# Attention values of five sequence halves loaded by GpSimd's queue, and the first operand pair read into another pool

## The chip, the cores and the metric

One core of a Trainium2 chip runs the whole program. The metric is the time of one execution in microseconds (us). The engines are named as in the profile: PE (TensorE matmul; PEld its weight loads), DVE (VectorE), ACT (ScalarE), POOL (GpSimd) and SP (SyncE, which here issues DMAs and computes nothing).

## What is computed

A block-local attention is followed by two feed-forward layers, all in float32 with a residual of the rounding carried in a second operand.

```
# q, k, v: [4, 8, 768, 64]; mem_k, mem_v: [4, 8, 8, 64]
for each chunk c of 32 queries:
    keys = 8 memory rows + 16 rows to the left + the chunk + 8 rows to the right
    a = softmax(q_c @ keys^T / 8);  out_c = a @ values        # per batch and head
x = out as [3072 tokens, 512]
h = x @ w_in;  g = h * clip(h + 3, 0, 6) / 6;  x = g @ w_out          # 512 -> 2048 -> 512
h = x @ w_in2; g = leaky_relu(h, 0.01);        out = g @ w_out2       # 512 -> 2048 -> 512
```

## The kernel before

**Attention.** The tokens are eight halves j = 0 to 7 of 384 tokens (half a batch's sequence). Each half has two units, `unit(j, quad, ...)`, of four heads. A unit loads queries and keys (`load_qk`, line 491, two DMAs of 448 KB), copies the keys into windows (`windows`), makes scores on PE (line 544), softmax on DVE and ACT, multiplies by the reciprocal of the sums (`norm`, line 598, on POOL or DVE), transposes on PE (line 602), and multiplies by the values on PE (line 634). The values are loaded by `load_v`: for each of two pairs of heads six DMAs, four of 84 KB (line 502) and two of 24 KB (line 504), in pieces of 512 bytes; so a unit has twelve such DMAs. Halves 0 and 1 are loaded in other forms (`load_whole`, `half_unit`). The result of a unit goes to operand tiles or, from half 2 on in part, through `attended` in memory (line 707).

**Feed-forward.** Tokens are blocks of 512. Blocks 0 and 1 are done plainly (lines 998 and 1047). The later blocks are taken in pairs, p = -2 and -1 for layer 1 and p = 0, 1, 2 for layer 2, by a scheme of seven products instead of eight (lines 1322 and 1490). `x_pair(p, ...)` makes the operands of a pair: `x_quarter` reads four tiles `b11`, `b12`, `b21`, `b22` (line 1126, `src`, 256 KB each) for each of two quarters, forms sums and differences on DVE, and splits each operand into two parts on ACT and DVE (lines 341 and 344, helpers `copy` and `minus`). For p = -2 the tiles come from `attended`.

**Places.** Tiles live in pools with a fixed number of places. Pool "w" has 33 places of 4 KB for each partition; weights, rings of kept sums (`kept1i` and others, line 1265), and operands share it. Pool "a" has 4 places; it holds queries and keys of halves 3 to 7, and for halves 6 and 7 also values and softmax tiles; `src` of `x_quarter` is there too. A load waits until a place is free.

**Order.** Every piece of work is a `Task` with a priority key and a cost for each engine that may do it. `schedule` simulates the engines with these costs and writes each engine's instructions in the order in which the simulation started them. On the chip each engine then runs its list in order, and waits on semaphores. So a cost or an engine that is changed for one task can change the order of everything behind it. For a DMA the planner takes 500 ns on SP and 1000 ns on POOL for each issue, and a landing later:

```
ISSUE = {"SP": 500.0, "POOL": 1000.0}
STARTS, LANDS, SURE = 1900.0, 500.0, 1500.0
...
                    for _ in range(pick.issues):
                        at = max(at, lanes[e].pop(0)) + ISSUE[e]
                        wire = max(wire, at + STARTS) + d / pick.issues
                        lanes[e].append(wire + LANDS)
...
                    push(wire + LANDS + (SURE if pick.allocs else 0.0), "done", (pick, e))
```

`norm` is offered to POOL first, and DVE takes it where POOL would end over 2.5 us later than DVE. In a unit from half 3 on, `load_v` comes after both `windows`; the loads of the next unit's queries and keys come after this unit's scores (halves 3 to 5, `ROOMY`) or after its first exponentials and both `load_v` (halves 6 and 7). Units of halves 6 and 7 begin after the last operand of `x_pair(-2)`.

Of the kernel before, what the change touches and what calls it, by code (L numbers as in the profile page):

```python
# [17 lines left out]
B, H, S, D, NMEM = 4, 8, 768, 64, 8  # L18
# [7 lines left out]
NC = G // CHUNK  # L26
# [30 lines left out]
RATE_QK, RATE, RATE_V, COLD = 380.0, 220.0, 300.0, 1.1  # L57
# [198 lines left out]
def tile_attn_moe_moe2(ctx: ExitStack, tc: tile.TileContext, raw, w1i, w1o, w2i, w2o, out):  # L256
    nc = tc.nc
# [24 lines left out]
    def make(b, kind=None):  # L282
        if b.tag in ("hx", "y") and b.tag not in pools:

            (attention if b.tag == "hx" else begin).close()
            pools[b.tag] = (ctx.enter_context(tc.tile_pool(name=b.tag, bufs=places[b.tag], space=PSUM, side="right" if b.tag == "hx" else "left")), [128, 512], F32)
        pool, shape, dt = pools[b.tag]
        if kind is not None:
            shape, dt = kind
        b.t = pool.tile(shape, dt, tag=b.tag, name=b.tag)  # L290
        return b.t
# [20 lines left out]
    def act(n, fixed=90.0):  # L312
        return fixed + 0.855 * n
# [13 lines left out]
    def dma(nbytes, rate=250.0):  # L327
        return nbytes / rate
# [3 lines left out]
    def add(fn, opts, key, **kw):  # L332
        t = Task(fn, opts, key, **kw)
        tasks.append(t)
        return t
# [129 lines left out]
    def unit(j, quad, key, tag, own=False, direct=False, loads=None):  # L465
# [7 lines left out]
        v = [Buf("w" if own or roomy else "a") for _ in range(2)]  # L473
        mx, s = Buf("mx"), Buf("mx")
        ps = pt = pv = Buf(tag)
        plain = own and j < 2
# [12 lines left out]
        def load_qk(i):  # L489
            def fn(eng):  # L490
                nc.sync.dma_start(out=make(qk[i], ([128, 2, QK], F32)), in_=both_groups(2 * quad + i))
            return fn

        def load_v(i):
            def fn(eng):
                make(v[i], ([128, 2, NC, 2 * D], F32))
                for par in range(2):
                    rows = of_raw(par, slice(0, KW), slice(QK, RAW))[i]
                    for g in range(2):
                        a = rows[g, NMEM:W]  # L500
                        there = bass.AP(tensor=a.tensor, offset=a.offset, ap=[a.ap[0], [CHUNK * a.ap[0][0], NC], a.ap[1]])
                        nc.sync.dma_start(out=v[i].t[par * D + NMEM:(par + 1) * D, g], in_=there)
                    mem = rows[0, :NMEM]
                    nc.sync.dma_start(out=v[i].t[par * D:par * D + NMEM].rearrange("r g c d -> r (g c) d"), in_=mem.unsqueeze(1).to_broadcast([NMEM, 2 * NC, 2 * D]))
            return fn

        def load_whole(i):

            def fn(eng):
                make(v[i], ([128, 6, 2 * D], F32))  # L510
                of = raw[b, 2 * quad + i, g0:g0 + 4, :, QK:RAW]
                nc.sync.dma_start(out=v[i].t[:, :4], in_=of.rearrange("g r d -> r g d"))
                for gp in range(2):
                    nc.sync.dma_start(out=v[i].t[gp * D:(gp + 1) * D, 4:], in_=of[2 * gp:2 * gp + 2, CHUNK:CHUNK + W].rearrange("g r d -> r g d"))
            return fn
# [198 lines left out]
        loads = loads or (key - 50, key - 50, key - 38, key - 38)  # L714
        l1 = [add(load_qk(i), {"SP": dma(128 * 2 * QK * 4, RATE_QK)}, loads[i], after=() if own else turn, allocs=[qk[i]]) for i in range(2)]
        t = [add(windows(i), ({"DVE": 850.0} if i or quad else {"ACT": 1050.0}) if j == 0 else {"ACT": 1050.0}, key - 30, after=[l1[i]], allocs=[kw[i]], uses=[qk[i]]) for i in range(2)]
        l2 = [add(load_whole(i) if plain else load_v(i), {"SP": dma(128 * 2 * NC * 512, RATE_V if plain else RATE)}, loads[2 + i], after=() if own else t, allocs=[v[i]], issues=3 if plain else 6, loads=plain) for i in range(2)]
        if plain:
            l2 = [add(memory(i), {"POOL": 1500.0}, key - 20, after=[l2[i]], uses=[v[i]]) for i in range(2)]
        t = marks["s", j, quad] = add(scores, {"PE": (COLD if direct else 1.0) * 1300.0}, key - 16, ins=192, after=t, allocs=[ps], uses=[*qk, *kw])  # L720
        scored = t
        if direct and quad in SHIFT:
            t = add(greatest, {"DVE": 2100.0}, key - 15, after=[t], allocs=[mx, e], uses=[ps])
            t = add(exp_all, {"ACT": act(2 * PAIRS * W)}, key - 13, after=[t], uses=[e])
            t = add(total, {"DVE": 1250.0}, key - 12, after=[t], allocs=[s], uses=[e])
        else:
            t = add(greatest, {"DVE": 1200.0}, key - 15, after=[t], allocs=[mx], uses=[ps])
            t = add(exp(0), {"ACT": 6 * 330.0}, key - 13, after=[t], allocs=[e, s], uses=[ps, mx])
            if not own:
                turn[:] = [scored] if roomy else [t, *l2]  # L730
            t = add(exp(1), {"ACT": 6 * 330.0}, key - 13, after=[t], uses=[ps, mx, e, s])
            t = add(total, {"DVE": 350.0}, key - 12, after=[t], uses=[s])
        t = add(norm, {"DVE": 900.0} if direct else {"POOL": 1800.0, "DVE": 900.0}, key - 11, after=[t], uses=[e, s])
        t = marks["t", j, quad] = add(transpose, {"PE": (COLD if direct else 1.0) * 600.0}, key - 7, ins=12, after=[t], uses=[e, ps])
        t = add(take_p, {"ACT": act(PAIRS * 128)}, key - 5, after=[t], uses=[pt, e])
        t = marks["v", j, quad] = add(values_whole if plain else values, {"PE": (COLD if direct else 1.0) * 1600.0}, key, ins=192, after=[t, *l2], uses=[e, *v, ps])
# [376 lines left out]
    def x_quarter(p, j, key, need):  # L1113


        a, b = pair_of(p)
        src = {n: Buf("a") for n in ("b11", "b12", "b21", "b22")}
        tt = Buf("w")
        ts = (tt, tt)
        got = {}  # L1120

        def load(n):
            t0 = blocks[a if n[2] == "1" else b][0]
            k = j + 2 * (n[1] == "2")
            r = src[n]
            got[n] = add(lambda e: nc.sync.dma_start(out=make(r, ([128, N], F32)), in_=spill[k, :, t0:t0 + N] if p >= 0 else attended[k, :, t0 - PLAIN * N:t0 - PLAIN * N + N]), {"SP": dma(N * 512, 330.0)}, key - 12, after=need[n[2] == "2"], allocs=[r])

        def sub(out, x, y, after, allocs=(), uses=()):
            return add(lambda e: minus(e, out(), x(), y()), {"DVE": dve(N)}, key, after=after, allocs=allocs, uses=uses)

        def parts_of(name, of, own, after):
            bufs = xop[p, name]
            first = xtask[p, name][0][:1], xtask[p, name][1][:1]
            hi = add(lambda e: copy(e, operand(p, name, 0, j).bitcast(F32R), of()), {"ACT": act(N)}, key, after=after + first[0], allocs=[] if first[0] else bufs[:1], uses=[own] + (bufs[:1] if first[0] else []))
            new = not first[1] and len(bufs) == 2
            lo = add(lambda e: minus(e, operand(p, name, 1, j).bitcast(F32R), of(), operand(p, name, 0, j).bitcast(F32)), {"DVE": dve(N)}, key, after=[hi] + first[1], allocs=bufs[1:] if new else [], uses=[own, bufs[0]] + ([] if new else bufs[1:]))
            xtask[p, name][0].append(hi)
            xtask[p, name][1].append(lo)
            return [hi, lo]

        def at(n):
            return lambda: src[n].t[:, :N]

        def t_at(i):
            return lambda: made(tt)[:, i]

        for n in src:
            load(n)

        def tt_kind():  # L1150
            for t in set(ts):
                make(t, ([128, 2, N], F32))

        def t_1(e):
            tt_kind()
            minus(e, t_at(0)(), src["b12"].t[:, :N], src["b11"].t[:, :N])

        d11 = parts_of("b11", at("b11"), src["b11"], [got["b11"]])
        if p >= 0:
            parts_of("b21", at("b21"), src["b21"], [got["b21"]])  # L1160
        t1 = add(t_1, {"DVE": dve(N)}, key, after=[got["b11"], got["b12"]], allocs=[*dict.fromkeys(ts)], uses=[src["b11"], src["b12"]])
        t2 = sub(t_at(1), at("b22"), t_at(0), [t1, got["b22"]], uses=[*ts, src["b22"]])
        parts_of("t2", t_at(1), ts[1], [t2])
        if p < 0:
            parts_of("b21", at("b21"), src["b21"], [got["b21"]])
        parts_of("t1", t_at(0), ts[0], [t1])
        t3 = sub(at("b12"), at("b22"), at("b12"), [t1, got["b22"]], uses=[src["b12"], src["b22"]])
        parts_of("t3", at("b12"), src["b12"], [t3])
        if p < 0 and j:
            key += 10  # L1170
        parts_of("b22", at("b22"), src["b22"], [got["b22"]])
        t4 = sub(at("b11"), at("b21"), t_at(1), [t2, t1, got["b21"], *d11], uses=[src["b11"], src["b21"], ts[1]])
        parts_of("t4", at("b11"), src["b11"], [t4])
# [404 lines left out]
    for f in range(KF):  # L1578
        for which, src, at in (("1i", w1i, pos_h["1", int(f >= KF // 2), f]), ("1o", w1o, pos_y["1", int(f >= KF // 2), f])):
            i = 2 * f + (which == "1o")  # L1580
# [33 lines left out]
    for kind, j, f, *n in seq2:  # L1614
        if kind == "p":
            p, i, n = j, f, n[0]
# [69 lines left out]
```

## Time and profile before

| | |
|---|---|
| median of 3 runs | 1046.41 us (1045.3 to 1048.34) |
| the profiled execution's own time | 1046.62 us |
| its span | 1044.8 us |
| PE busy | 1029.5 us, 99% of the span |
| DVE, ACT, POOL busy | 856.0, 694.8, 23.9 us (82%, 67%, 2%) |
| DMA | 220.50 MB, all but instruction fetches through one queue, 63.2% of 16 engines' span |

The span is the time from the first to the last instruction; the execution's own time is 1.8 us longer. A stretch's busy time is read against its length: what is missing is time in which that engine stood still. All DMAs of the kernel before are issued by SP; their issue instructions are not counted as busy.

### The profile page before, as it was taken

How to read it: one execution, taken by the hardware profiler on the slowest of the kernel's cores; microseconds unless marked ns; L12 is line 12 of the kernel's file. 1: busy time of each engine (PE TensorE's matmuls, PEld its weight loads, DVE VectorE, ACT ScalarE, POOL GpSimd, SP SyncE). 2: the span in 40 equal slices, each digit the busy share in tenths (PEclk: the TensorE clock that was granted, in tenths of full speed). 3: DMA queues.
4: the chain of work that ended last, by engine and by line, in shares of the span. 5: the costliest groups of instructions: out<-in, count | busy, mean ns of one | idle time of the engine just before them, and what ended most of it. 6: DMA issues, size and time to landing. Idle time of an engine off the chain costs nothing.

```text
span 1044.8 us, 20156 instructions
## 1 busy us (share of the span) xinstructions
PE 1029.5 (99%) x7476; PEld 846.7 (81%) x7476; DVE 856.0 (82%) x1422; ACT 694.8 (67%) x1478; POOL 23.9 (2%) x31
## 2 busy tenths in 40 slices
PE   7999999999999999999999999999999999999998
PEld 4788888877888888888888888888888888888887
DVE  6995897578998778699999898999476998566775
ACT  4886776555988554576786576776565874666753
POOL 3010000000000000000000000000000000000000
PEclk9999999999999999999999999999999999999999
DMA  9989787776888888664647884446342554432451
GB/s 259 298 237 323 256 286 236 247 256 215 276 288 292 292 279 278 245 217 127 212 135 268 291 286 162 147 158 218 117 167 81 177 194 153 169 114 95 148 181 61
DMA packets 127315, 220.50 MB, mean 211 GB/s; under 512 B 12528, under 2 KB 76016, under 8 KB 127216
## 3 DMA queue, kind: packets, MB, share of 16 engines
q1 hardware_dynamic: 127216, 219.20, 63.2%
q8 instruction: 59, 0.97, 0.4%
q14 instruction: 40, 0.33, 0.1%
HBM read 156.24 MB, written 62.91 MB: 210 GB/s over the span
## 4 chain that ended last, share of the span: by engine, by line
PE 85%; DMA 6%; DVE 4%; ACT 2%; SPq 2%; issue 1%; DVEq 0%; ACTq 0%
PE y L1322 17%; PE y L1490 12%; PE h L1322 11%; PE y L1047 10%; PE h L1490 8%; PE hx L1322 8%; PE hx L1490 8%; PE h L998 3%; PE h L1047 2%; DMA w<-in_raw 2%; DMA kept1i<-ys 1%; DMA a<-in_raw 1%; PE at L634 1%; DMA half<-ys 1%; PE at L544 1%
## 5 line engine op out<-in xcount | busy, mean ns | idle before, releaser
L344 DVE TENSOR_TENSOR w<-w 128x512 fp32r<-128x512 f32 (+2 forms) x393 | 323.3, 858 | 29.0 <-ACT w L341 28.4
L341 ACT CAST w<-w 128x512 fp32r<-128x512 f32 (+1 forms) x290 | 223.7, 805 | 12.5 <-DMA w<-floats 3.9
L1047 PE MATMUL y<-g,w 128*128 128x512 f32 (+1 forms) x540 | 124.9, 375 | 1.5 <-ACT g L341 0.6
L1322 PE MATMUL y<-w 128*128 128x512 f32 x516 | 124.2, 389 | 0.0
L1322 PEld LDWEIGHTS y<-w 128*128 128x128 f32 x516 | 96.7, 188 | 20.1
L1047 PEld LDWEIGHTS y<-g,w 128*128 128x128 f32 x540 | 94.0, 188 | 19.9 <-ACT g L341 1.4
L1490 PE MATMUL y<-w 128*128 128x512 f32 x384 | 90.3, 389 | 0.0
L341 ACT CAST g<-w 128x512 fp32r<-128x512 f32 x80 | 49.7, 623 | 58.3 <-PE y L1490 22.5
L1490 PEld LDWEIGHTS y<-w 128*128 128x128 f32 x384 | 72.1, 188 | 15.0
L1296 ACT ACTIVATE w<-w 128x512 f32<-128x512 f32 x72 | 45.3, 633 | 43.9 <-DVE w L1289 21.5
L998 PE MATMUL h<-xh,w 128*128 128x512 f32 (+1 forms) x288 | 66.0, 370 | 0.0
L344 DVE TENSOR_TENSOR g<-w,g 128x512 fp32r<-128x512 f32 x80 | 54.4, 689 | 11.5 <-ACT g L341 11.4
L1490 PE MATMUL h<-w 128*128 128x512 f32 x264 | 62.1, 389 | 0.0
L1322 PE MATMUL h<-xl,w 128*128 128x512 f32 x240 | 58.3, 391 | 1.2 <-ACT xl L341 1.2
L1490 PE MATMUL hx<-w 128*128 128x512 f32 x252 | 59.2, 389 | 0.0
L1490 PEld LDWEIGHTS h<-w 128*128 128x128 f32 x264 | 49.5, 188 | 10.3
L998 PEld LDWEIGHTS h<-xh,w 128*128 128x128 f32 x288 | 49.7, 188 | 9.0
L1490 PEld LDWEIGHTS hx<-w 128*128 128x128 f32 x252 | 47.3, 188 | 9.8
L1322 PEld LDWEIGHTS h<-xl,w 128*128 128x128 f32 x240 | 44.8, 188 | 11.3 <-ACT xl L341 1.6
L1322 PE MATMUL y<-xh,w 128*128 128x512 f32 x216 | 51.9, 389 | 0.0
L1367 DVE TENSOR_TENSOR w<-y,w 128x512 f32<-128x512 f32 x35 | 23.9, 687 | 29.9 <-PE y L1322 27.1
L1322 PEld LDWEIGHTS y<-xh,w 128*128 128x128 f32 x216 | 40.5, 188 | 8.5
(242 smaller groups left out, 1847.7 us busy)
## 6 DMA issues: line engine op xcount, KB each, us to landing
w<-kept2i SPq DMA_DIRECT2D x42, 512.0 KB
w<-kept2o SPq DMA_DIRECT2D x42, 512.0 KB
w<-kept1i SPq DMA_DIRECT2D x28, 512.0 KB
a<-in_raw SPq DMA_DIRECT2D x20, 448.0 KB
w<-in_w1i SPq DMA_DIRECT2D x16, 512.0 KB
w<-in_w1o SPq DMA_DIRECT2D x16, 512.0 KB
w<-in_w2i SPq DMA_DIRECT2D x16, 512.0 KB
w<-in_w2o SPq DMA_DIRECT2D x16, 512.0 KB
```

Of the source, the lines that this page charges most:

```text
L341: nc.scalar.copy(out, in_) if e == "ACT" else engine(e).tensor_copy(out=out, in_=in_)
L344: engine(e).tensor_tensor(out=out, in0=a, in1=b, op=ALU.subtract)
L544: nc.tensor.matmul(ps.t[h * CHUNK:(h + 1) * CHUNK, par, i * W:(i + 1) * W], qk[h // 2].t[r, gp, (h % 2) * G + c * CHUNK:(h % 2) * G + (c + ...
L634: nc.tensor.matmul(pv.t[(h % 2) * D:(h % 2 + 1) * D, par, (h // 2) * 2 * G + i * CHUNK:(h // 2) * 2 * G + (i + 1) * CHUNK], v[h // 2].t[r, ...
L998: nc.tensor.matmul(h.t[:, o:o + n], w.t[:, 1 if p == 1 else 0, k * 128:(k + 1) * 128], x[:, k, c0:c0 + n], start=(p == 0 and k == 0 and o ...
L1047: nc.tensor.matmul(bank(banks[d])[:, c0:c0 + n], w.t[:, 1 if p == 1 else 0, d * 128:(d + 1) * 128], g.t[:, 1 if p == 2 else 0, at:at + n], ...
L1296: return add(lambda e: nc.scalar.activation(out=at(), in_=at(), func=AF.Prelu, alpha=0.01), {"ACT": act(N)}, key, after=[after], uses=uses)
L1322: nc.tensor.matmul(bank(to), wt(l, o)[:, kt * 128:(kt + 1) * 128].bitcast(F32R), operand(p, name, 1 if q == 2 else 0, kt).bitcast(F32R), s ...
L1367: done[2] = add(lambda e: nc.vector.tensor_tensor(out=half_of(x, 0), in0=bank(bb), in1=ut.t[:, 0], op=ALU.add), low, key, after=[k, done[1 ...
L1490: nc.tensor.matmul(bank(to[d]), wt(1 if q == 1 else 0, o)[:, d * 128:(d + 1) * 128].bitcast(F32R), g.t[:, 1 if q == 2 else 0], start=(fres ...
```

## The change

Two edits. In units from half 3 on (`j >= 3 and not plain`; ten units, 120 DMAs) the two `load_v` tasks are issued by POOL, and the planner is told so: engine POOL, 1000 ns an issue, a rate of 300 bytes per ns on the wire instead of 220, and POOL counted as free after its last issue. In `x_quarter`, the four tiles of pair p = -2 take places of pool "w" instead of pool "a". The order is planned anew with both.

```diff
+        by_pool = j >= 3 and not plain
+
         def load_v(i):
...
-                        nc.sync.dma_start(out=v[i].t[par * D + NMEM:(par + 1) * D, g], in_=there)
+                        (nc.gpsimd if by_pool else nc.sync).dma_start(out=v[i].t[par * D + NMEM:(par + 1) * D, g], in_=there)
                     mem = rows[0, :NMEM]
-                    nc.sync.dma_start(out=v[i].t[par * D:par * D + NMEM].rearrange("r g c d -> r (g c) d"), in_=mem.unsqueeze(1).to_broadcast([NMEM, 2 * NC, 2 * D]))
+                    (nc.gpsimd if by_pool else nc.sync).dma_start(out=v[i].t[par * D:par * D + NMEM].rearrange("r g c d -> r (g c) d"), in_=mem.unsqueeze(1).to_broadcast([NMEM, 2 * NC, 2 * D]))
...
-        l2 = [add(load_whole(i) if plain else load_v(i), {"SP": dma(128 * 2 * NC * 512, RATE_V if plain else RATE)}, loads[2 + i], after=() if own else t, allocs=[v[i]], issues=3 if plain else 6, loads=plain) for i in range(2)]
+        l2 = [add(load_whole(i) if plain else load_v(i), {"POOL" if by_pool else "SP": dma(128 * 2 * NC * 512, RATE_V if plain or by_pool else RATE)}, loads[2 + i], after=() if own else t, allocs=[v[i]], issues=3 if plain else 6, loads=plain or by_pool) for i in range(2)]
...
-        src = {n: Buf("a") for n in ("b11", "b12", "b21", "b22")}
+        src = {n: Buf("w" if p < -1 else "a") for n in ("b11", "b12", "b21", "b22")}
```

## Rows read from the trace of the kernel before

**Rows 1.** Windows over five stretches: length, busy us of each engine, clock, DMA.

```profile
0.00:78.00 78.00, 69.81 (x1081) 51.67 (x1082) 65.60 (x150) 57.12 (x193) 14.11 (x25) 0.98 0.88 264
78.00:250.00 172.00, 169.59 (x2190) 142.53 (x2189) 130.09 (x248) 110.93 (x345) 3.31 (x2) 1.00 0.82 271
250.00:365.00 115.00, 113.72 (x1224) 92.86 (x1223) 103.28 (x181) 89.06 (x238) 6.50 (x4) 1.00 0.81 268
365.00:1014.00 649.00, 649.00 (x2865) 537.37 (x2864) 537.55 (x815) 425.46 (x684) 0.00 (x0) 1.00 0.55 184
1014.00:1044.80 30.80, 27.34 (x121) 22.32 (x119) 19.48 (x30) 12.27 (x20) 0.00 (x0) 1.00 0.25 96
```

**Rows 2.** Waits of PE, 78 to 1014 us: total us, times, longest.

```profile
PE h L1322 <- ACT xl L341: 1.2, 1, 1.2
PE at L602 <- DVE w L598: 0.9, 1, 0.9
PE y L1047 <- ACT g L341: 0.6, 1, 0.6
PE y L1047 <- DVE g L344: 0.4, 1, 0.4
PE y L1047 <- ACT ys L1077: 0.4, 1, 0.4
```

**Rows 3.** Timeline of SP, 215 to 262 us: start, us, instruction.

```profile
221.50 1.88 SPq L1126 DMA_DIRECT2D a<-attended  x4
...
232.33 2.73 SPq L1126 DMA_DIRECT2D a<-attended  x3
235.15 1.33 SPq L1265 DMA_DIRECT2D w<-kept1i  x3
...
247.52 0.32 SPq L1126 DMA_DIRECT2D a<-attended  x1
```

**Rows 4.** Timelines of DVE and ACT, 244 to 256 us; idle before in brackets.

```profile
252.26 0.69 DVE L1080 SCALAR_TENSOR_TENSOR ys<-y,ys 128x512 f32<-128x512 f32 x1 [2.79 <-PE y L1047]
...
254.29 0.69 DVE L344 TENSOR_TENSOR w<-a,w 128x512 f32<-128x512 f32 x1
...
255.01 0.62 ACT L341 CAST xl<-w 128x512 fp32r<-128x512 f32 x1 [1.38 <-DVE w L344]
```

**Rows 5.** Lines 502 and 504: ns of an issue (least, median, most), first and last start.

```profile
L502 SPq DMA_DIRECT2D a<-in_raw x32: 315/400/1880, 272.6 to 356.5; - x32
...
L504 SPq DMA_DIRECT2D a<-in_raw x16: 308/320/1018, 273.4 to 356.9; - x16
```

**Rows 6.** Timelines of SP and PE around two units' value loads.

```profile
196.15 0.92 SPq L502 DMA_DIRECT2D w<-in_raw  x2
...
213.40 0.81 PE L634 MATMUL at<-w 64*64 64x32 f32 x40
...
272.57 0.80 SPq L502 DMA_DIRECT2D a<-in_raw  x2
...
278.22 0.32 SPq L504 DMA_DIRECT2D a<-in_raw  x1
...
285.61 1.62 PE L634 MATMUL at<-a 64*64 64x32 f32 x96
```

**Rows 7.** Timeline of all engines, 332 to 334.5 us.

```profile
332.37 1.47 POOL L598 TENSOR_TENSOR a<-a,mx 128x768 f32<-128x768 f32 x1 [24.38 <-DMA a<-in_raw]
332.74 1.39 DVE L400 TENSOR_SCALAR wm<-wm 128x512 uint32<-128x512 uint32 x1
```

**Rows 8.** DVE by line and form, 78 to 365 us: busy us, mean ns.

```profile
L400 DVE TENSOR_SCALAR wm<-wm 128x512 uint32<-128x512 uint32 x16 | 7.5, 481 | 0.4 <-ACT wm L396 0.4
...
L400 DVE TENSOR_SCALAR ys<-ys 128x512 uint32<-128x512 uint32 x8 | 3.4, 421 | 2.1 <-ACT ys L396 2.1
...
L400 DVE TENSOR_SCALAR st<-st 128x512 uint32<-128x512 uint32 x8 | 3.3, 422 | 0.0
```

**Rows 9.** Timeline of SP, 364 to 400 us.

```profile
366.28 0.37 SPq L707 DMA_DIRECT2D attended<-a  x1
397.23 0.63 SPq L1126 DMA_DIRECT2D a<-attended  x1
```

## The prediction

> **What bounds the kernel now.** I read the windows first [rows 1], because busy shares of a whole run hide where an engine is needed. PE is busy for 649.00 of 649.00 us between 365 and 1014 us, at full granted clock; nothing that only changes loads can shorten that stretch. PE stands still for 78 − 69.81 = 8.19 us at the start, 172 − 169.59 = 2.41 us from 78 to 250, 115 − 113.72 = 1.28 us from 250 to 365, and 30.80 − 27.34 = 3.46 us at the end; another 1046.62 − 1044.8 = 1.82 us of the execution lie outside the span. The start holds the first halves, whose loads stay on SP, and the end is the last products' way out; both edits act after that start and before 365 us. So 2.41 + 1.28 = 3.69 us is all the PE time that they can win, while their loss has no such bound.
>
> Next the waits of PE in that stretch [rows 2]: five, together 3.5 us, none of them for a DMA. The longest, 1.2 us, is for ACT writing a part of an operand in "xl". To see what that ACT waited for I followed the timelines of DVE and ACT back [rows 4]: ACT had stood idle 1.38 us for DVE, and DVE formed the difference from an "a" tile only at 254.29, after it had waited 2.79 us, in order, for a PE result that the instruction ahead of it needed. The tile itself came late: SP read the first four `attended` tiles together at 221.50, three more from 232.33 on, and the eighth at 247.52 [rows 3], since pool "a" has four places.
>
> **The operands in pool "w".** The edit removes the wait for places of "a": eight reads can go out together, so the eighth is issued up to 247.52 − 221.50 = 26 us earlier. DVE can then form the difference before 252.26, in the 2.79 us in which it stood still [rows 4]. The wait of 1.2 us goes. From nothing (the planner leaves DVE's order as it is) to 1.2 us is the gain; I take 1.2, because the instruction that PE waited for hangs on just this read. The cost is eight places of "w" for some 25 us, in the stretch in which SP fetches `kept1i` for the first products of the pair, at 235.15 [rows 3]. If those are kept back as the tiles were, by 232.33 − 221.50 = 10.8 us, PE can stand for anything from 0 to 10.8 us. I take 0: 33 places hold more than the rings and the operands named in the code at that point, and the planner places the loads by key; the other end is a rival.
>
> **Off SP's queue.** Ten units lose 8 issues of line 502 and 4 of line 504 each. At their medians [rows 5] that is 80 × 0.400 + 40 × 0.308 = 44 us of SP's time. Everything that was behind them in SP's list (weights, rings, stores) can go out earlier, some 4.4 us in each unit. That is worth nothing by itself, because no wait of PE ends on a DMA [rows 2]; the bound above nothing is the other four waits, 3.5 − 1.2 = 2.3 us, if ACT and DVE were late for SP's sake.
>
> **On POOL's queue.** No row shows a DMA issued by POOL. The nearest below is SP's own issue, 0.31 to 0.40 us [rows 5]; above, POOL's whole multiply of 128x768, 1.47 us [rows 7]. I take 1.0 us, between these ends, which is also the cost the planner lays the order out with. What decides is not the cost but its excess over the plan, and the plan can be worked out from the lines quoted above. Twelve issues at 1.0, then 1.9 to start, 0.2 for the last piece (393,216 bytes at 300 a ns, in six), 0.5 to land and 1.5 in reserve are 16.1 us from a unit's first value load to the earliest values on PE. With 1.9 + 0.5 for the landing, PE waits only if an issue takes over (16.1 − 2.4) / 12 = 1.14 us. Up to there POOL's slowness is hidden by PE's feed-forward products, which the planner puts in front of the values.
>
> Does that postponement cost anything? On SP the same sum was 6 + 1.9 + 0.3 + 2 = 10.2 us, so a unit's values come 5.9 us later. In half 5 there was room: first load 196.15, values 213.40, which is 17.25 us [rows 6]. In half 6 it was 285.61 − 272.57 = 13.04, and the next unit's queries wait for the values there, so the four units of halves 6 and 7 are pushed by up to 4 × 5.9 = 23.6 us. Their last store leaves at 366.28, and the next reads of `attended` start at 397.23 [rows 9]: 366.28 + 23.6 = 389.9, still 7.3 us before. PE does not run dry meanwhile, because the products of the pair p = -2 fill it already. I count 0; the cover ends if the four units are pushed by over 397.23 − 366.28 = 30.95 us together.
>
> A rule of the Trainium skill speaks against this edit: "SBUF — State Buffer", in the section "SBUF: two separate sides", says that descriptors of a DMA issued by GpSimd cannot be written while DVE runs in a mode that takes both ports. By it the delay would come from DVE's single-input operations; no row here shows a DMA so delayed. In rows: line 400 is such an operation, 32 times with 7.5 + 3.4 + 3.3 = 14.2 us from 78 to 365 us [rows 8]. If all of that lay in front of POOL's 120 issues, an issue would take 1.0 + 0.12 = 1.12 us, just inside 1.14. So this alone leaves the sum as it is, but nothing to spare.
>
> **The softmax multiply.** The norm of six of the ten units ran on POOL: two and four instructions in the two stretches [rows 1]. With POOL taken for 12 us, the planner gives most of them to DVE. That is about even for DVE: beside POOL's multiply a DVE instruction of line 400 took 1.39 us instead of 0.42 [rows 7, 8], a loss of 0.97, and on DVE itself 768 elements cost about 1.03 (0.69 for 512 [rows 4], times 1.5). DVE has 42 us of slack from 78 to 250 and 11.7 from 250 to 365 [rows 1]. I count 0.
>
> **A new order.** Both edits change what the planner sees, so the other four waits, 2.3 us, will sit elsewhere. I keep them at 2.3; 0 to twice that is the bound.
>
> **Sum.** 1046.62 − 1.2 = 1045.4 us for the profiled execution. Its time was 0.21 us over the median of the runs, 1046.41, so the forecast is 1045.2 us. 0.3% (3.1 us) is about what a measurement of this kernel can tell from no change; the forecast lies within it.
>
> **Rivals.**
>
> *All of PE's standing time goes.* Weights that leave SP earlier let ACT and DVE start earlier, and all 3.69 us vanish: 1042.7. For it: SP's list is in order and value loads stand in it. Against: the waits are for ACT and DVE, and neither is named as waiting for SP.
>
> *Nothing is won.* The 1.2 us is handed on, because DVE still runs in order behind a PE result, or the new order makes as many waits as it removes: 1046.4, and up to 1048.7 with 2.3 more. This is also the case that the edit doesn't do what it says.
>
> *POOL's issue takes more than 1.14 us.* Then PE waits at line 634 in each of ten units, since its list is in order. At 1.3 us it is 10 × 12 × 0.16 = 19 us (1065), at 1.47 us 40 us (1086). For it: 168 pieces of 512 bytes are much for one issue, and with the 0.12 above 1.02 us by itself is enough. Against: that a DMA issue is shorter than POOL's multiply is likely where SP needs a third of that.
>
> *POOL's issuing holds DVE up.* POOL's multiply did so, by 0.97 us [rows 7]. If an issue did the same, 48 issues would take 47 us from DVE between 250 and 365 us, where it has 11.7: 35 us late, 1081. It decides from 11.7 / 48 = 0.24 us an issue on. Against: an issue reads and writes no tile, the multiply streams three.
>
> *Places of "w" run short.* The ring is late by half of 10.8 us and PE stands for it: 1046.4 + 5.4 = 1051.8.
>
> **How the numbers follow.** Chances: forecast 0.56, all gone 0.10, nothing won 0.10, POOL's issue 0.12, DVE held up 0.05, places 0.07. Over 3.1 us faster are the second and a part of the first (0.08): 0.18. Over 3.1 us slower are the last three and the edges of the first and third (0.02 each): 0.28. Within 0.3%: 0.54. The forecast's own range, with the other waits from 0 to twice 2.3 us, is 1042.9 to 1047.5. The range that leaves out 2 in 10 goes from 1042.4 to 1052.0: below is almost nothing, since 3.69 us is all there is; above remain the cases of POOL and DVE, 0.17, and a part of the places.
>
> **What would show it.** Right: lines 502 and 504 on POOL with a median near 1.0 us; all eight reads of `attended` into "w" before 235 us; no wait of PE for ACT "xl"; norms on DVE; units of halves 6 and 7 some 6 us longer, their last store before 397 us; PE idle 2.3 to 2.5 us between 78 and 365. Wrong: PE waits at line 634 for a DMA; line 400 or two-input DVE operations longer beside POOL's issues; PE waiting for `kept1i`; or PE idle after 365 us. The clock was 1.00 throughout that stretch [rows 1] and no edit leaves PE without work, so I expect no change there.

## The result, and the profile after

The changed kernel takes 1054.48 us (median of 6 runs, 1051.2 to 1055.5) against 1046.76 us for the kernel before (6 runs, 1044.45 to 1048.73): ratio 1.0071, 95% interval 1.0057 to 1.0085. It is slower by 7.7 us, above the range that was forecast. The profiled execution took 1054.44 us with a span of 1052.6 us. From line 502 on, line numbers are two higher than before.

The windows of the changed kernel, for the stretches of [rows 1]:

```profile
0.00:78.00 78.00, 70.23 (x1085) 52.25 (x1086) 65.03 (x150) 57.31 (x193) 15.92 (x28) 0.98 0.87 266
78.00:250.00 172.00, 163.08 (x2148) 137.99 (x2147) 124.57 (x239) 109.25 (x341) 49.29 (x73) 0.97 0.79 260
250.00:365.00 115.00, 115.00 (x1146) 94.49 (x1145) 106.52 (x188) 88.90 (x238) 30.31 (x48) 1.00 0.85 264
365.00:1014.00 649.00, 648.71 (x2950) 537.27 (x2949) 532.91 (x812) 421.19 (x682) 0.15 (x1) 1.00 0.55 185
1014.00:1052.60 38.60, 34.89 (x154) 28.56 (x153) 27.03 (x40) 16.20 (x27) 0.00 (x0) 1.00 0.31 109
```

From 250 to 365 us PE no longer stands still: 1.28 us are won. From 78 to 250 us it stands 172 − 163.08 = 8.92 us, where it stood 2.41: 6.51 us are lost. With small differences elsewhere (−0.42, +0.29, +0.25) standing time grows by 5.35 us. PE's busy time over the span grows as well, from 1029.46 to 1031.91 us, by 2.45 us. 5.35 + 2.45 = 7.80 us is the whole difference of the spans. The second term can't be read closer than that: two traces of one and the same program further below differ by 3.4 us in PE's busy time (1031.2 and 1027.8 us).

The waits of PE from 78 to 1014 us; compare [rows 2]:

```profile
PE at L604 <- ACT ys L1079: 4.4, 1, 4.4
PE at L546 <- issue: 2.7, 1, 2.7
PE y L1049 <- DVE g L344: 1.1, 1, 1.1
PE y L1049 <- issue: 0.7, 1, 0.7
PE at L636 <- DMA a<-in_raw: 0.3, 1, 0.3
```

The wait for ACT's "xl" is gone; a wait of 4.4 us is new. It stands at the transposes of unit (2,1), which is not one of the ten units that were edited. ("issue" is time in which the profile shows nothing that the engine waited for.) The chain of waits from 76 to 106 us (start, us, what) leads to its cause:

```profile
82.14 10.98 DMA attended<-w
...
93.22 3.65 ACT w L582 x24
96.87 0.58 ACT r L1015
97.45 0.98 ACT ys L1079 x2
98.43 0.10 issue
98.54 1.51 PE at L604 x6
```

```profile
93.22 0.31 ACT L582 ACTIVATE w<-at,mx 128x64 f32<-128x64 f32 x1 [8.09 <-DMA attended<-w]
```

ACT stood 8.09 us at the exponentials of unit (2,1) for a store to `attended` (128 KB) that took 10.98 us to land. Why should exponentials wait for a store? In the built program their tile lies at the address of the softmax tile of unit (2,0), which this store reads. In the kernel before it lies at another address, and its exponentials waited for DVE alone. (In the built programs of four runs further below, the tile lies at the stored tile's address in the run with POOL's queue and the old order, and at the address of the kernel before in those with the new order on SP, from half 4 on, and with the freed place.) There the same store went out later, behind value loads. Rows of SP, and then of ACT, kernel before:

```profile
74.68 0.49 SPq L439 DMA_DIRECT2D halves<-w  x1
75.69 1.54 SPq L502 DMA_DIRECT2D w<-in_raw  x2
...
89.80 0.39 SPq L707 DMA_DIRECT2D attended<-w  x1
```

```profile
88.20 0.32 ACT L580 ACTIVATE w<-at,mx 128x64 f32<-128x64 f32 x1 [2.28 <-DVE mx L565]
```

SP of the kernel after, in the same stretch, without the twelve value loads of unit (3,0) between them:

```profile
74.27 3.01 SPq L439 DMA_DIRECT2D halves<-w  x3
80.97 0.33 SPq L393 DMA_DIRECT2D w<-in_w1i  x1
82.14 0.37 SPq L709 DMA_DIRECT2D attended<-w  x1
```

So 82.14 instead of 89.80, and five stores of `halves` (512 KB each, two of them before the first row) ahead of it where there had been three. The place in memory of a tile is chosen while the program is built, among those that are free by then. In the program of the kernel after the store stands well ahead of these exponentials, in that of the kernel before shortly ahead of them, and the place was handed on in the first only; that the earlier store is the reason is argued from this.

From 80 to 94 us the DMA engines ("the wire" from here on) were full in the kernel after and had gaps in the kernel before; the last but one column is their share, kernel after first:

```profile
80.00:94.00 14.00, 14.00 (x232) 12.18 (x224) 4.28 (x9) 3.08 (x11) 3.79 (x6) 1.00 1.03 383
```

```profile
80.00:94.00 14.00, 14.00 (x255) 12.11 (x255) 6.23 (x13) 8.09 (x35) 0.00 (x0) 1.00 0.81 249
```

PE's speed behind the two long stands, in windows of the kernel after (columns as in [rows 1]; the third last is the granted clock, then the DMA share):

```profile
94.00:96.00 2.00, 0.12 (x2) 0.00 (x0) 0.00 (x0) 2.00 (x15) 0.00 (x0) 1.00 1.04 424
96.00:98.50 2.50, 0.00 (x0) 0.00 (x0) 1.47 (x4) 2.50 (x10) 0.00 (x0) 0.61 1.00 410
98.50:100.00 1.50, 1.46 (x7) 1.49 (x8) 0.55 (x2) 1.50 (x4) 0.00 (x0) 0.50 0.97 376
100.00:104.00 4.00, 4.00 (x29) 3.87 (x29) 3.41 (x7) 3.11 (x6) 0.00 (x0) 0.58 0.47 177
104.00:108.00 4.00, 4.00 (x117) 3.96 (x117) 3.28 (x8) 3.31 (x9) 0.00 (x0) 1.00 0.12 32
...
128.00:131.00 3.00, 0.34 (x25) 0.27 (x21) 0.89 (x2) 0.00 (x0) 0.14 (x1) 0.94 1.06 356
131.00:134.00 3.00, 3.00 (x29) 2.44 (x14) 1.95 (x5) 1.19 (x9) 2.03 (x4) 0.50 1.06 317
```

0.50 is 1.2 of the 2.4 GHz. PE stood still, the granted clock fell, and PE was busy for 1.46 + 4.00 + 3.00 = 8.46 us at about half speed. By the clocks of these three rows that costs 1.46 × 0.50 + 4.00 × 0.42 + 3.00 × 0.50 = 3.9 us (an estimate); the busy time of the whole span grew by 2.45 us only, and why by no more was not taken apart. The store of 128 KB took its 10.98 us while the DMA share was 1.03; a run below has one that landed in 2.0 us behind a share of 0.45.

POOL's issues of halves 3 to 5, by line: ns of one (least, median, most). Those of halves 6 and 7 have the same medians.

```profile
L504 POOL DMA_DIRECT2D w<-in_raw x48: 657/662/863, 76.0 to 203.2; - x48
```

```profile
L506 POOL DMA_DIRECT2D w<-in_raw x24: 583/583/818, 77.5 to 203.8; - x24
```

An issue on POOL takes 0.58 to 0.66 us, well under the 1.14 us from which it would have decided.

### The profile page after: what moved, and what is told of

It reads as the page before. It is cut to its first block, busy times and chain, and to the rows that moved or that the text cites. A ratio compares the mean times of both kernels' runs of the same rounds, so it can differ in the third digit from the quotient of the medians.

```text
span 1052.6 us, 20244 instructions
## 1 busy us (share of the span) xinstructions
PE 1031.9 (98%) x7476; PEld 850.6 (81%) x7476; DVE 856.1 (81%) x1425; ACT 692.8 (66%) x1478; POOL 95.7 (9%) x148
## 4 chain that ended last, share of the span: by engine, by line
PE 93%; DMA 2%; ACT 2%; issue 1%; DVE 1%; POOL 1%; SPq 0%; POOLq 0%; ACTq 0%; DVEq 0%
PE y L1324 17%; PE y L1049 13%; PE y L1492 12%; PE h L1324 11%; PE h L1492 8%; PE hx L1492 8%; PE hx L1324 8%; PE h L1000 7%; PE h L1049 2%; PE at L636 2%; PE at L546 1%; DMA attended<-w 1%; PE at L604 1%; PE ac L461 1%; DMA a<-in_raw 1%
## 5 line engine op out<-in xcount | busy, mean ns | idle before, releaser
L344 DVE TENSOR_TENSOR w<-w 128x512 fp32r<-128x512 f32 (+2 forms) x407 | 332.8, 856 | 32.2 <-ACT w L341 31.9
L341 ACT CAST w<-w 128x512 fp32r<-128x512 f32 (+1 forms) x296 | 226.3, 799 | 11.8 <-PE hx L1492 2.9
```

The costliest lines, as they stand in the source:

```text
L341: nc.scalar.copy(out, in_) if e == "ACT" else engine(e).tensor_copy(out=out, in_=in_)
L344: engine(e).tensor_tensor(out=out, in0=a, in1=b, op=ALU.subtract)
```

## Experiments

Two questions were open at first: is it the new order of instructions that costs, or POOL's queue itself, and which of the two edits? Each ratio is taken against runs of the kernel before that were measured beside it (medians 1045.69, 1047.69 and 1046.68 us in the three groups), so ratios compare better than times.

**POOL's queue, old order.** Only the engine that issues is changed; the planner is told nothing.

```diff
-                        nc.sync.dma_start(out=v[i].t[...], in_=there)
+                        (nc.gpsimd if j >= 3 else nc.sync).dma_start(out=v[i].t[...], in_=there)
```

(line 504 likewise)

> All engines keep the order of the kernel before; only the 120 value DMAs of halves 3 to 7 leave SP's list for POOL's, at the same places. Order theory (the loss comes from the order laid out anew, in which the exponentials of half 2's second unit take a place that half 2's first store to attended frees only 11 us after its issue): 1045 to 1048 us, PE idle 78 to 250 us at most 4 us, no wait of PE over 2 us in that stretch. Queue rival (loads on a ring of their own hold up SP's transfers and PE's instruction fetch): 1050 us or more, with waits of 2.5 us and more as in the changed kernel.

Measured: 1063.71 us, ratio 1.0157 (1.0134 to 1.018). The order theory's 1045 to 1048 us fell: the new order is not needed for a loss. PE waited for POOL's norms (6.8 us) and others:

```profile
PE at L602 <- POOL a L598: 6.8, 3, 2.5
PE y L1047 <- issue: 2.9, 2, 2.7
PE at L602 <- ACT ys L1077: 1.3, 1, 1.3
```

Here too the tile of unit (2,1) had got the place of the stored one, and its exponentials waited 4.99 us for the store.

**New order, SP's queue.** The kernel after, with the planner still told "POOL", but the DMAs issued by SP.

```diff
-                        (nc.gpsimd if by_pool else nc.sync).dma_start(out=v[i].t[...], in_=there)
+                        nc.sync.dma_start(out=v[i].t[...], in_=there)
```

> All engines keep the order of the changed kernel; only the 120 value DMAs go back to SP's list, at the places where they were planned. Order theory: the wait of ACT for the store to attended near 85 to 93 us stays (5 us or more) and with it a PE wait of 3 us or more before the transposes of half 2's second unit; 1051 us or more. Queue rival: the store lands within some 4 us of its issue, PE's wait there is under 1 us, 1043 to 1047 us.

Measured: 1053.49 us, ratio 1.0058 (1.0042 to 1.0075). As slow as the kernel after, but not for the same reason: the exponentials of unit (2,1) didn't wait. SP's list, laid out as if the value loads weren't in it, sent the stores of "ys" tiles to `half` in memory at 99.51 us (before: 95.07), and ACT, which writes their places next, waited 6.47 us for one of them (its row names a store to `attended`, the built program has the wait on `half<-ys`):

```profile
108.06 1.45 ACT L396 ACTIVATE ys<-w 128x512 f32<-128x512 f32 x2 [6.47 <-DMA attended<-w]
```

PE then stood 6.2 us at 118 us, waiting for ACT's "g". A run like this changes one thing and breaks another; it does not isolate the cause.

**Each edit alone.** First POOL with `src` left in pool "a", then the kernel before with only the `src` edit.

```diff
-        src = {n: Buf("w" if p < -1 else "a") for n in ("b11", "b12", "b21", "b22")}
+        src = {n: Buf("a") for n in ("b11", "b12", "b21", "b22")}
```

> The first edit alone, planned anew; the operand tiles of pair p = -2 stay in pool a. Order theory: the stretch to 200 us is that of the changed kernel, with its PE waits of about 4.4 and 2.7 us, and the operand wait near 250 us is back at up to 1.3 us: 1054 to 1057 us. Rival (the operand tiles in pool w cost the time): 1044 to 1048 us.

Measured: 1053.44 us, ratio 1.0055 (1.0038 to 1.0073), just below what the order theory gave. The waits are there, but shorter than in the kernel after: ACT 6.3 us for the store, PE 2.2 us behind it and 1.8 us on "issue".

> The second edit alone, planned anew; all loads on SP. Order theory and the prediction's step for this edit: the PE wait for xl near 254 us (1.2 us) is gone, the waits before 220 us stay, 1043.5 to 1046 us. Rival (operand tiles in pool w cost the time): 1050 us or more, with PE waiting after 220 us.

Measured: 1044.44 us, ratio 0.9999 (0.9977 to 1.0021): no difference that these ten runs can tell. The loss comes with the first edit, the move to POOL's queue, and not with the second.

**Where on POOL's queue.** Two parts of the edit, `by_pool` from half 4 on, and for half 3 only; and the kernel after with one instruction more, which keeps the stored tile's place out of reach until the exponentials of unit (2,1) are done:

```diff
-        by_pool = j >= 3 and not plain
+        by_pool = j >= 4 and not plain
```

> The kernel after, with the values of half 3 left on SP's queue; halves 4 to 7 (96 of 120 DMAs) stay on POOL's, and the operands stay in pool w. Up to about 110 us each engine's order and each place in memory is then that of the kernel before. Place theory (the loss begins where POOL takes the values of half 3 from SP in the saturated stretch from 75 us on, the attended store of unit (2,0) goes out 7.7 us earlier, and its place is handed to the exponentials of unit (2,1), which then wait for the store): no wait of ACT for the attended store near 93 us, no stall of PE near 94 us, clock 1.00 there, and 1044 to 1047.5 us. Queue theory (a second queue costs by itself, wherever it is used, in proportion to its DMAs): 96/120 of 7.7 us are left, 1052 to 1053 us.

Measured: 1046.98 us, ratio 0.9999 (0.9981 to 1.0016). ACT had no wait for the store near 93 us, PE waited 2.9 us in all from 78 to 1014 us, and its clock was 1.00. With 96 of the 120 DMAs on POOL's queue, but with the `src` edit in it too, the kernel is as fast as the kernel before.

```diff
-        by_pool = j >= 3 and not plain
+        by_pool = j == 3 and not plain
```

> The kernel after, with only half 3's values (24 of 120 DMAs) on POOL's queue. Place theory: the exponentials of unit (2,1) again take the place of the attended store of unit (2,0) and wait for it, so nearly the whole loss is there, 1050 to 1054 us. Queue theory: 24/120 of 7.7 us, 1047 to 1049 us.

Measured: 1056.36 us, ratio 1.0084 (1.0068 to 1.01); ACT waited 8.68 us for the store and PE 4.9 us behind it:

```profile
94.91 0.31 ACT L582 ACTIVATE w<-at,mx 128x64 f32<-128x64 f32 x1 [8.68 <-DMA attended<-w]
```

The 24 DMAs of half 3 make the whole loss, and somewhat more than was expected.

```diff
-        e = Buf("w" if own or roomy else "a")
+        e = first_e[j, quad] = Buf("w" if own or roomy else "a")
...
+                if gp and (j, quad) == (2, 1):
+                    nc.scalar.activation(out=begun, in_=first_e[2, 0].t[:, 0, 0, :1], func=AF.Exp)
```

> The kernel after, with one more instruction: ACT reads one column of the softmax tile of unit (2,0) after the exponentials of unit (2,1), so that their tile must take another place (the one that it has in the kernel before) and doesn't wait for the attended store. Every engine's order is otherwise that of the kernel after. Place theory: no wait of the exponentials for a DMA, no stall of 4.4 us of PE near 94 us and no lower clock behind it; with the stall on instructions near 128 us left, 1047 to 1049.5 us. Rival (the wire is what is late, and the next wait takes over): ACT waits instead for the stores of half from ys before it splits the next weights, as in the run with the new order on SP, PE stands for 4 to 6 us some 15 to 25 us later, 1052 to 1055 us.

Measured: 1046.6 us, ratio 1.0 (0.9986 to 1.0014), with 120 DMAs on POOL and every other instruction in the order of the kernel after. The waits of PE, and ACT's first exponential:

```profile
PE at L547 <- issue: 3.3, 2, 2.7
PE y L1052 <- DVE g L345: 1.1, 1, 1.1
PE y L1052 <- ACT g L342: 0.9, 1, 0.9
```

```profile
90.26 0.32 ACT L583 ACTIVATE w<-at,mx 128x64 f32<-128x64 f32 x1 [2.99 <-DVE mx L568]
...
93.74 0.27 ACT L588 ACTIVATE begun<-w 128x1 f32<-128x1 f32 x1
```

The store's wait, the 4.4 us stand and the low clock are gone together (granted clock 1.00 from 78 to 250 us; in this trace it is 1.00 in the first 78 us too, where the kernel after has 0.98); the rival, that the next wait takes over, is not seen: ACT waited 0.65 us for `half<-ys`, and PE not at all for it. One instruction of 0.27 us takes the ratio from 1.0071 back to 1.0000.

That is the time of the kernel before, not the best that is to be had: this run and the one from half 4 on also hold the `src` edit, which alone is at 0.9999 above and at 0.9974 below. Whether POOL's queue costs up to some 2.7 us besides the place stays open; this trace has 3.3 us of "issue" waits that the trace with `src` alone has not.

**The converse.** The kernel before, all DMAs on SP, no order changed, but the tile of unit (2,1) put into the stored tile's place.

```diff
-                    make(e, ([128, 2, PAIRS, W] if plain else [128, PAIRS, 2, W], F32))
+                    if (j, quad) == (2, 1):
+                        e.t = first_e[2, 0].t
+                    else:
+                        make(e, ([128, 2, PAIRS, W] if plain else [128, PAIRS, 2, W], F32))
```

> The kernel before, all DMAs on SP, with one thing changed: the softmax tile of unit (2,1) is put into the place of the softmax tile of unit (2,0), whose attended store leaves at 89.8 us, instead of into a place that was free long before. No engine's order is changed. Place theory: the exponentials of unit (2,1) wait until that store has landed, 5 to 11 us after its issue, 94.8 to 100.8 us instead of 88.2; PE stands 6 to 12 us near 95 us and the granted clock falls behind it; 1053 to 1062 us, though POOL issues no DMA at all. Rival (the loss belongs to POOL's queue or to the new order): within 2 us of the kernel before.

Measured: 1049.72 us, ratio 1.0025 (1.0009 to 1.0042). Slower, by the same mechanism and without POOL, but less than expected. SP's issue, ACT's first exponential, and two windows:

```profile
91.33 0.39 SPq L711 DMA_DIRECT2D attended<-w  x1
```

```profile
93.34 0.31 ACT L584 ACTIVATE w<-at,mx 128x64 f32<-128x64 f32 x1 [6.04 <-DMA attended<-w]
```

```profile
88.00:92.00 4.00, 4.00 (x40) 3.76 (x30) 1.23 (x4) 0.00 (x0) 0.00 (x0) 1.00 0.45 110
...
96.00:100.00 4.00, 1.64 (x11) 1.46 (x10) 1.96 (x4) 4.00 (x15) 0.00 (x0) 0.87 1.03 420
```

Here the store landed 93.34 − 91.33 = 2.0 us after its issue, on a wire that was at 0.45 from 88 to 92 us; I had expected 5 to 11. PE stood 2.4 us. So the place makes the wait. Its length goes with what lies ahead on the wire, as far as these two cases show: 2.0 us here, 10.98 us in the kernel after, for the same 128 KB.

**What else the old order cost on POOL.** The first run lost 17 us; were it the norms that stood behind POOL's loads? They are moved to DVE, and in a second kernel the place is kept free as well.

```diff
-            engine(eng).tensor_tensor(out=ev(), in0=ev(), in1=sf.unsqueeze(2)...
+            engine("DVE" if j >= 3 else eng).tensor_tensor(out=ev(), in0=ev(), in1=sf.unsqueeze(2)...
```

> The run with POOL's queue and the old order, with the norms of halves 3 to 7 moved from POOL to DVE at the same point of the order. Theory that the norms stood behind POOL's value loads: the waits of PE for POOL's norm, 6.8 + 0.8 us, go, and about 1055 to 1057 us are left of 1063.7. Rival: DVE has no room at these points and hands the wait on, over 1060 us.

Measured: 1066.69 us, ratio 1.0191 (1.0151 to 1.023). The theory falls. The waits for POOL's norms are gone, and others have taken their place:

```profile
PE at L634 <- DMA a<-in_raw: 9.1, 5, 3.0
PE at L602 <- DVE w L598: 3.0, 2, 2.1
```

The values themselves land too late for a PE list that was laid out for SP's issues. The four runs lie far apart (two near 1062.5, two near 1071 us).

> The same, and the softmax tile of unit (2,1) kept out of the place of the attended store by the extra read of one column. If the norms and the place are both what made POOL's queue dear under the old order, the 1.3 us stall and the lower speed behind it go as well and 1048 to 1053 us are left; if the second queue costs by itself, no more than 2 us are won against the run beside it.

Measured: 1061.27 us, ratio 1.0135 (1.0111 to 1.0159). Neither of the two came. The medians are 5.4 us apart, but two of the four runs beside this one are as fast as its slowest two; the traces say it more clearly: from 78 to 250 us PE stands 172 − 170.47 = 1.53 us instead of 172 − 164.79 = 7.21. 14.6 us are left against the kernel before, in which the trace shows 7.9 us of waits for late values and a clock of 0.96 from 250 to 365 us; the rest was not taken apart.

**The better version.** The `src` edit alone, in more runs.

> The kernel before with the operands in pool w alone, measured in more rounds. By its trace it wins the 1.2 us for which PE waited for the operand's low part: ratio 0.9988. Rival: the wait is handed on, ratio 1.000.

Measured: 1043.95 us against 1046.68, ratio 0.9974 (0.9959 to 0.9988): by a quarter of a per cent faster than the kernel before in these runs, where the first ten had shown 0.9999 (0.9977 to 1.0021). Its windows and its only wait of PE from 78 to 1014 us:

```profile
78.00:250.00 172.00, 170.98 (x2200) 144.55 (x2199) 133.27 (x254) 115.14 (x357) 3.30 (x2) 1.00 0.82 272
250.00:365.00 115.00, 115.00 (x1234) 94.55 (x1233) 103.38 (x182) 86.68 (x232) 5.03 (x3) 1.00 0.85 278
```

```profile
PE at L602 <- DVE w L598: 0.9, 1, 0.9
```

PE stands 1.02 us where it stood 3.69. In the trace of the first runs of the same program it stood 1.72 us, since it waited 0.7 us for ACT's "g" at 195 us; from 250 to 365 us it was busy throughout in both.

## Why the prediction was wrong

**What bounds the kernel** was read rightly: neither stretch after 365 us changed its standing time by over 0.3 us, and all that could be won was standing time before it. That the loss has no such bound was said too, and that is where it went.

**The operands in pool "w"**: right. The eight reads go out together, 229.44 to 233.94 us (the eighth 13.6 us earlier than before, where 26 was the bound), and the wait for "xl" is gone. Alone the edit takes the standing time from 3.69 to 1.02 us in one trace and to 1.72 in the other, 2.0 to 2.7 us instead of 1.2. 1.28 of that is the stretch from 250 us on, where the operands are; that the small waits near 112 and 212 us are gone as well was not foreseen, and why was not tried.

**Off SP's queue**: this is the step that failed. It said that what stood behind the value loads could go out earlier, and that this was "worth nothing by itself, because no wait of PE ends on a DMA". It was weighed as a gain only. (Its 44 us take 0.308 for line 504's median, which is the least; with 0.320 they are 44.8, and nothing hangs on it.) The value loads, which wait for places themselves, had paced SP's list. Without them the stores of 512 KB went out in a row, the wire was full from 80 to 94 us (share 1.03, before 0.81), and the small store behind them went out 7.7 us earlier and took 10.98 us to land; its place, handed on while the program was built, tied ACT to that landing for 8.09 us and PE to ACT for 4.4. That no wait of PE ended on a DMA was true of the places as they had been given out.

**A new order** then carried the wrong number: I kept the other waits at 2.3 us with twice that as the bound, and PE's waits came to 4.4 + 2.7 + 1.1 + 0.7 + 0.3 = 9.2 us. And "no edit leaves PE without work, so I expect no change" of the clock fell with it: PE did stand without work, and the clock was at 0.50 to 0.61 from 96 to 104 us and at 0.50 from 131 to 134.

**POOL's queue**: right on the side that decides. With 0.66 and 0.58 us instead of 1.0 the twelve issues took 8 × 0.66 + 4 × 0.58 = 7.6 us, and PE waited 0.3 us in all for a value. Under the old order, without the planner's postponement, PE waited at line 634 for a value: 1.2 us in the first such run, 9.1 and 7.9 us in the two with the norms on DVE. The last store of halves 6 and 7 left at 374.02 us (up to 389.9 was allowed) and the next reads of `attended` started at 401.55. The rule of the Trainium skill that spoke against the edit ("SBUF — State Buffer", section "SBUF: two separate sides") is not borne out here in the size that the prediction allowed for, 1.12 us an issue: with line 400 on DVE as before, no issue of the 120 took over 0.863 us. By what another page of the Trainium skill states ("Trainium Kernel Development and Optimization", section "Key Constraints"), that queues of several engines share the DMA engines and only the time of issuing is saved, the edit had little to win; the trace agrees, with the DMA share at 1.03 from 80 to 94 us, where both queues were in use.

**The softmax multiply**: right in its zero. DVE was busy for 856.06 us (856.0 before). The four of halves 6 and 7 went to DVE, at 0.95 us each (1.03 estimated); POOL kept three between 78 and 250 us, so "most of them" was half of them.

**The rivals.** POOL's issue over 1.14 us, DVE held up, and places of "w" running short didn't come. The last was nearest, since a place of "w" did decide, but not for being scarce: in the run with the freed place the tile found another one, and the time was back at the kernel before. No rival had that.

## What to carry to other kernels

Loads in an in-order queue also pace what stands behind them: before moving them to another queue, ask what will then go out sooner, whether the wire is full there, and whose place comes free in another sequence. A wait that a tile inherits from its place can be found in the row of the instruction that writes it (an exponential that waits for a store), and can be tested with one small read that keeps the place occupied. Try the edits of a change one by one: here one of the two did no harm alone, and in the larger of two sets of runs won 2.7 us, and it was buried under the other.

## What had not been expected of the hardware

PE stood still in the middle of 96 like matmuls, with "issue" as the only cause that the profile names: 75 at 127.08 us, then 2.66 us nothing, then 21:

```profile
130.73 0.64 PE L546 MATMUL at<-w,a 64*32 64x64 f32 x21 [2.66 <-issue]
```

The same stand is in the runs with POOL alone (1.82), half 3 alone (2.66), SP with the new order (2.16) and the freed place (2.72). In the run with POOL's queue and the old order, and in that with the norms on DVE, there is a stand on "issue" of 2.65 and 2.93 us before matmuls of line 1047. The DMA share was 0.97 to 1.06 around it in the kernel after, and 0.97 from 122 to 127 us in the freed-place run. In the kernel before, in the run from half 4 on and in that of the operands alone PE has no wait from 78 to 1014 us that ends on "issue". What it waited for was not tried and stays open; that the fetching of its instructions is held up on a full wire, a rival in the first expectation, is neither shown nor excluded.

Stands of about the same length were followed by different granted clocks: 0.50 after 2.66 us in the kernel after, 1.00 after 2.72 us in the freed-place run, 0.87 and then 0.70 around and after 2.36 us in the converse run. The length of a single stand doesn't settle it here.
